# A fixed order for the first triangular inversion and the Gram products around it

## The chip, the cores and the metric

The kernel runs on one core of a Trainium2 chip. The metric is the device time of one execution in microseconds, the median of three runs. Engines are named TensorE (PE), VectorE (DVE), ScalarE (ACT), GpSimd (POOL) and SyncE (SP, which issues the DMAs).

## The reference

Three stages follow each other. The first is a gated delta rule over 768 tokens, for 4 batches of 8 heads with 48 features:

```
k_n = k / (|k| + 1e-6)
for t in range(768):
    y[t]  = q[t] @ state
    v_old = k_n[t] @ state
    state = state + beta[t] * outer(k_n[t], v[t] - v_old)
```

The outputs, 3072 tokens of 384 features, go through two dense blocks: `elu(x @ w_in) @ w_out`, and the same with a rational function P(h)/Q(h) in place of elu. The weights of both blocks arrive as float64 and are converted on the chip.

## The kernel before

**Windows.** The sequence is cut into 12 chunks of 64 tokens; two chunks make a window, so there are 6. For a window the kernel computes Gram products of keys and queries (`g_item`, line 270: four TensorE products into one of three PSUM buffers of the pool `pa`, a masked multiply on VectorE at L282 that keeps the query part, three copies on ScalarE at L286 to L288 that keep the key part; eight items per window). From the key part it inverts 32 x 32 triangular systems on VectorE (`t_pieces`): a transpose of the Gram matrix (L297, am<-gd), small steps on norms and beta (L301 to L333), 15 row steps, then four block steps px0 to px3 and four steps pt0 to pt3, each a product into `tmp` (L345) and a reduce (L346), and at the end a transpose (L372, tp_t<-tt). Then the recurrence over the chunks (`chain`) takes its turn: GpSimd multiplies tp_t with beta (L432, tb), TensorE solves (L460, L471, L483), ScalarE and VectorE copy and subtract (L463, L475, L488).

**Weights.** A conversion (`conv_x`, `conv_d`, `conv_s`) turns half a row block of float64 into fp32: two ScalarE steps (L160, L162), one or two VectorE steps (L176 to L179), a sign step on ScalarE (L180), a multiply on GpSimd (L182); for the first block's input weights a split follows on ScalarE (L71) and GpSimd (L72). There are two ce buffers between these steps, and eight raw buffers between the load (L142) and the conversion; a raw buffer is loaded again when GpSimd has done L182.

**Dense blocks.** For each window the first block runs its 16 slices (h_a at L578 to L580, o at L596 to L598), beside the next window's recurrence; behind the last window comes the second block.

**What sets the order.** Every piece is entered in a list with a number, its place in time: `at(t, fn)`. The list is sorted, and the pieces are emitted in that order. Pieces below `Q["ma"]` are emitted in a section whose order is kept on each engine, pieces above are handed to a scheduler that orders them by readiness under its own costs and puts them on the engines' queues, also between those of the fixed section. Window 0's Grams stand at -99 to -92, its inversion from -90 to -49, window 1's Grams from -72.1 to -63.3, the first conversions and the first recurrence from -48, -47 on. In before `ma` is -200, and nothing is below it.

Of the kernel before, what the change touches and what calls it, by code (L numbers as in the profile page):

```python
# [26 lines left out]
HD = DM // 2  # L27
NV = 15
Q = dict(
    ma=-200, xo=2.244, pg0=0, pg1=2, ca=0, g1=-72.135, g1d=1.259, t1a=-33.632, t1b=-8, npre=3, c0=-47,  # L30
    c0d=4.533, c1=-1.042, c1r=4.439, b1=0.704, c1o=0.919, h0=1.013, h0d=0.5, h1=0.586, h1d=0.462, g2=-7.824,
    g2d=1.116, g3w1=-0.578, g3=-0.806, t2=2.578, t2b=14.166, t3b=9, p=14.315, tm=4, chd=1.061, ws=0.808,
    sx=-0.529, ev=16.5, c5=1.1, c5d=0.4, l5=1.3, wu0=0, wl0=2, wd0=5, wy0=2, wm0=2, wu1=6, wl1=7, wd1=6, wy1=0,
# [4 lines left out]
def kernel(  # L38
# [520 lines left out]
    def g_list(w):  # L559
        return [(lambda j=j, s=s, b=b: g_item(j, s, b)) for j, s in enumerate(WINS[w]) for b in range(4)]  # L560
# [195 lines left out]
    def at(t, fn, *a):  # L756
        ev.append((t, len(ev), fn, a))

    def spread(t0, t1, fns, cost=None):
        cost = cost or [1.0] * len(fns)  # L760
        c = 0.0
        for fn, d in zip(fns, cost):
            at(t0 + (t1 - t0) * c / sum(cost), fn)
            c += d
# [33 lines left out]
    def t_at(w, t0, t1, t2, t3):  # L798
        tp = t_pieces(w)
        at(t0, tp[0])  # L800
        at(t0 + .3, tp[1])
        el = [4 * k * k for k in range(1, 8)] + [16 * k for k in range(8, 16)] + [1024, 768, 512, 256] + [256, 512, 768, 1024]
        spread(t1, t2, tp[2:-1], [.4 + .0021 * n for n in el])
        at(t3, tp[-1])
# [8 lines left out]
        at(-99 + i, fn)  # L813
    at(-91, chain_loads)
    at(10, coefs)
    t_at(0, -90, -85, -50, -49)
    for i, fn in enumerate(g_list(1)):
        at(Q["g1"] + Q["g1d"] * i, fn)
    at(-55, load_beta, 1)
# [8 lines left out]
    for w in range(NW):  # L828
# [15 lines left out]
        if w + 1 < NW:  # L844
            c0, cd = (Q["h0"], Q["h0d"]) if w == 0 else (Q["h1"], Q["h1d"])
# [150 lines left out]
```

## Time and profile before

| | |
|---|---|
| median of three runs | 1138.27 us (1136.64 to 1140.21) |
| the profiled execution | 1129.3 us, span 1127.5 us |
| TensorE busy | 1037.9 us, 92% of the span |
| VectorE busy | 904.5 us, 80% |
| ScalarE busy | 771.7 us, 68% |
| GpSimd busy | 466.4 us, 41% |

The profiled execution is shorter than the three timed ones; durations below are from it. A busy TensorE is not a TensorE at its peak, since the ends of its products are modelled. The share of busy time is a mean over stages: in the first 60 us TensorE is mostly idle and VectorE nearly full. An idle time in brackets is the time in which an engine waited in front of that row, with what ended the wait.

### The profile page before, as it was taken

The numbers are of one execution on the slowest core, as the hardware profiler recorded it, in microseconds if no ns is written. First come the engines' busy times: TensorE is split into PE (matmuls) and PEld (weight loads), VectorE is DVE, ScalarE is ACT, GpSimd is POOL, SyncE is SP. The second block draws the span as 40 slices with busy tenths as digits, with TensorE's granted clock in tenths as the row PEclk, the third lists the DMA queues.
The fourth block names the chain that finished last, engine by engine and source line by source line (L and its number), as shares of the span: only waits on it lengthen the run. The fifth ranks groups of instructions, "written<-read, shape, count | busy, mean of one in ns | idle before, by whom it ended". The sixth has DMA issues, their size and how long they took to land.

```text
span 1127.5 us, 20636 instructions
## 1 busy us (share of the span) xinstructions
PE 1037.9 (92%) x7952; PEld 835.8 (74%) x7952; DVE 904.5 (80%) x1240; ACT 771.7 (68%) x1525; POOL 466.4 (41%) x399
## 2 busy tenths in 40 slices
PE   7178898889798999899999999999999999999997
PEld 7155676667676778777888878778788888888885
DVE  4989889689857873795434379999999999999997
ACT  5568687866577546665665689976767667676764
POOL 1376655434332322242332145446363544536342
PEclk8559899999899989998999999999999999999999
DMA  9436343454364113120212044400100001010000
GB/s 287 155 102 200 116 147 114 131 161 126 97 189 149 59 50 121 60 81 1 81 49 62 1 148 133 120 28 1 56 1 25 32 1 56 1 56 1 29 1 28
DMA packets 51842, 91.75 MB, mean 81 GB/s; under 512 B 7072, under 2 KB 29728, under 8 KB 51744
## 3 DMA queue, kind: packets, MB, share of 16 engines
q1 hardware_dynamic: 51744, 90.43, 25.8%
q8 instruction: 62, 1.02, 0.4%
q14 instruction: 36, 0.29, 0.1%
HBM read 77.83 MB, written 12.58 MB: 80 GB/s over the span
## 4 chain that ended last, share of the span: by engine, by line
PE 54%; DVE 24%; ACT 7%; issue 6%; DMA 5%; POOL 3%; SPq 0%; ACTq 0%; DVEq 0%; POOLq 0%
PE o L733 13%; PE h_a L578 6%; PE h_a L579 6%; PE h_a L580 6%; DVE tmp L345 5%; PE o L596 3%; PE o L597 3%; PE o L598 3%; PE h_b L578 2%; PE h_b L579 2%; PE h_b L580 2%; DMA raw<-w_out 2%; DVE tt L346 2%; PE gp L279 2%; DVE wo L695 2%
## 5 line engine op out<-in xcount | busy, mean ns | idle before, releaser
L710 POOL TENSOR_TENSOR gl<-wo 128x1024 fp32r<-128x1024 f32 x47 | 147.3, 3134 | 202.4 <-DVE wo L709 174.2
L72 POOL TENSOR_TENSOR wor<-wo,wor 128x384 fp32r<-128x384 f32 x96 | 109.1, 1137 | 268.0 <-ACT wor L71 260.3
L578 PE MATMUL h_a<-xh,wi 128*128 128x512 f32 x417 | 173.9, 417 | 10.1 <-ACT pe L608 8.8
L579 PE MATMUL h_a<-xl,wi 128*128 128x512 f32 x417 | 168.9, 405 | 3.7 <-DVE xl L397 3.7
L580 PE MATMUL h_a<-xh,wi 128*128 128x512 f32 x417 | 167.8, 402 | 0.0
L733 PE MATMUL o<-gh,wo 128*128 128x512 f32 x564 | 135.9, 390 | 0.4 <-ACT ys L741 0.4
L613 DVE SCALAR_TENSOR_TENSOR e<-e,pe 128x512 f32<-128x512 f32 x96 | 70.8, 737 | 75.4 <-ACT e L609 75.1
L733 PEld LDWEIGHTS o<-gh,wo 128*128 128x128 f32 x564 | 105.2, 188 | 23.8 <-ACT ys L741 2.4
L596 PE MATMUL o<-gh,wor 128*128 128x512 f32 x288 | 115.8, 410 | 0.0
L597 PE MATMUL o<-gl,wor 128*128 128x512 f32 x288 | 114.5, 398 | 1.2 <-DVE gl L621 1.2
L598 PE MATMUL o<-gh,wor 128*128 128x512 f32 x288 | 113.0, 392 | 0.0
L578 PEld LDWEIGHTS h_a<-xh,wi 128*128 128x128 f32 x417 | 80.8, 194 | 30.5 <-ACT pe L608 10.9
L621 DVE TENSOR_TENSOR gl<-e,gh 128x512 fp32r<-128x512 f32 x88 | 79.2, 900 | 29.3 <-ACT gh L619 28.9
L579 PEld LDWEIGHTS h_a<-xl,wi 128*128 128x128 f32 x417 | 81.3, 195 | 22.1 <-DVE xl L397 7.2
L607 ACT ACTIVATE e<-h_a 128x512 f32<-128x512 f32 x91 | 54.2, 596 | 58.6 <-PE h_a L580 58.2
L580 PEld LDWEIGHTS h_a<-xh,wi 128*128 128x128 f32 x417 | 81.1, 194 | 17.3
L696 ACT ACTIVATE wo<-wo 128x1024 f32<-128x1024 f32 (+1 forms) x49 | 51.3, 1046 | 60.4 <-DVE wo L695 60.4
L619 ACT ACTIVATE gh<-e 128x512 fp32r<-128x512 f32 x96 | 60.0, 625 | 35.0 <-DVE e L613 35.0
L695 DVE SCALAR_TENSOR_TENSOR wo<-wo 128x1024 f32<-128x1024 f32 (+1 forms) x49 | 73.1, 1492 | 4.5 <-ACT wo L688 4.4
L71 ACT ACTIVATE wor<-wo 128x384 fp32r<-128x384 f32 x96 | 50.4, 525 | 35.7 <-PE o L598 35.3
L733 PE MATMUL o<-gl,wo 128*128 128x512 f32 x282 | 71.7, 389 | 0.8 <-POOL gl L710 0.8
L707 DVE SCALAR_TENSOR_TENSOR gh<-wo,ab_sb 128x1024 fp32r<-128x1024 f32 (+1 forms) x49 | 65.5, 1336 | 6.6 <-ACT wo L697 0.6
(168 smaller groups left out, 2462.8 us busy)
## 6 DMA issues: line engine op xcount, KB each, us to landing
kv<-c_kv SPq DMA_DIRECT2D x24, 576.0 KB, 4.6
gin<-g_in SPq DMA_DIRECT2D x69, 192.0 KB, 2.9
kq<-c_kq SPq DMA_DIRECT2D x22, 512.0 KB, 3.8
raw<-w_out SPq DMA_DIRECT2D x42, 192.0 KB, 2.5
raw<-w_in SPq DMA_DIRECT2D x34, 192.0 KB, 2.4
wo<-w_in SPq DMA_DIRECT2D x30, 192.0 KB, 2.7
xr<-x2d SPq DMA_DIRECT2D x6, 768.0 KB, 5.3
out_t<-ys SPq DMA_DIRECT2D x18, 256.0 KB, 2.2
```

The costliest lines, as they stand in the source:

```text
L72: eng.tensor_tensor(out=t[:, 1], in0=src, in1=t[:, 0].bitcast(F32), op=ALU.subtract)
L578: mm(out=ps, lhsT=hi, rhs=xh[:, c, 0:NC], start=(c == 0), stop=False)
L579: mm(out=ps, lhsT=hi, rhs=xl[:, c, 0:NC], start=False, stop=False)
L580: mm(out=ps, lhsT=lo, rhs=xh[:, c, 0:NC], start=False, stop=(c == 2))
L596: mm(out=ps[:, 0:NC], lhsT=hi[:, cs], rhs=gh[:, 0:NC], start=(f == 0), stop=False)
L597: mm(out=ps[:, 0:NC], lhsT=hi[:, cs], rhs=gl[:, 0:NC], start=False, stop=False)
L598: mm(out=ps[:, 0:NC], lhsT=lo[:, cs], rhs=gh[:, 0:NC], start=False, stop=(f == NF - 1))
L613: nc.vector.scalar_tensor_tensor(out=e, in0=e, scalar=-1.0, in1=p, op0=ALU.add, op1=ALU.add)
L621: eng.tensor_tensor(out=gl[:, 0:NC], in0=e, in1=gh[:, 0:NC].bitcast(F32), op=ALU.subtract)
L695: v.scalar_tensor_tensor(out=sq, in0=sq, scalar=1.0 + 1e-6, in1=ab, op0=ALU.add, op1=ALU.add)
L710: (v if k == NK - 1 else nc.gpsimd).tensor_tensor(out=gl, in0=sq, in1=ab, op=ALU.mult)
L733: mm(out=ps, lhsT=wo2[2 * j + i][:, int(p == 1), cs], rhs=(gl if p == 2 else gh)[:, n], start=(j == 0 and p == 0 and i == 0), stop=(j == N ...
```

## The change

Two numbers change. `ma` moves from -200 to -49.5, so that everything placed below -49.5 is emitted in the section with the kept order: the start, both windows' Grams, the first loads, and the first inversion. Its last piece, the transpose to tp_t, moves from -49 to -49.6, so that it is inside as well. Conversions and the recurrence stay with the scheduler.

```
-    ma=-200, xo=2.244, ...
+    ma=-49.5, xo=2.244, ...
...
-    t_at(0, -90, -85, -50, -49)
+    t_at(0, -90, -85, -50, -49.6)
```

VectorE, among the row steps of window 0's inversion, in before: L345 and L346 are its products and reduces (the last numbers are their sizes), L282 the masked multiply of a Gram item of window 1.

```order
L345 TENSOR_TENSOR tmp<-tt,am 128x64
L346 TENSOR_REDUCE tt<-tmp 128x4x4
L282 TENSOR_TENSOR p<-gp,cm_sb 128x256
L345 TENSOR_TENSOR tmp<-tt,am 128x100
L346 TENSOR_REDUCE tt<-tmp 128x4x5
L345 TENSOR_TENSOR tmp<-tt,am 128x144
L346 TENSOR_REDUCE tt<-tmp 128x4x6
L282 TENSOR_TENSOR p<-gp,cm_sb 128x256
L345 TENSOR_TENSOR tmp<-tt,am 128x196
```

The same place now:

```order
L345 TENSOR_TENSOR tmp<-tt,am 128x100
L346 TENSOR_REDUCE tt<-tmp 128x4x5
L345 TENSOR_TENSOR tmp<-tt,am 128x144
L346 TENSOR_REDUCE tt<-tmp 128x4x6
L345 TENSOR_TENSOR tmp<-tt,am 128x196
```

Seven of the eight multiplies of window 1 stood among the small steps and the row steps; now none does before the last row step (240 elements).

VectorE, from the third block step (px2, 512 elements) to the fourth (px3, 256) and on, in before: L179 is a conversion.

```order
L179 SCALAR_TENSOR_TENSOR ce<-wo_94 128x192
L346 TENSOR_REDUCE xx_t<-tmp 128x64
L179 SCALAR_TENSOR_TENSOR ce<-wo_94 128x192
L345 TENSOR_TENSOR tmp<-tt,am 128x256
L346 TENSOR_REDUCE xx_t<-tmp 128x64
L179 SCALAR_TENSOR_TENSOR ce<-wo_94 128x192
L345 TENSOR_TENSOR tmp<-xx_t,tt 128x256
L346 TENSOR_REDUCE tt<-tmp 128x16x4
L282 TENSOR_TENSOR p<-gp,cm_sb 128x256
```

The same place now, from the last multiply on:

```order
L282 TENSOR_TENSOR p<-gp,cm_sb 128x256
L345 TENSOR_TENSOR tmp<-tt,am 128x256
L179 SCALAR_TENSOR_TENSOR ce<-wo_94 128x192
L346 TENSOR_REDUCE xx_t<-tmp 128x64
L297 STREAM_TRANSPOSE am<-gd 128x1024
L345 TENSOR_TENSOR tmp<-xx_t,tt 128x256
L301 TENSOR_SCALAR x<-am 128x32
L179 SCALAR_TENSOR_TENSOR ce<-wo_94 128x192
L346 TENSOR_REDUCE tt<-tmp 128x16x4
```

The eight multiplies now stand from the 240-element row step to the 256-element block step, the last of them in front of the latter; four conversions stand in front of it in place of five. Window 1's transpose (L297) follows at once.

VectorE, around the end of the inversion (L372, tp_t), in before: L313 to L323 are window 1's small steps.

```order
L346 TENSOR_REDUCE tt<-tmp 128x16x4
L315 TENSOR_SCALAR t_432<-t_432 128x32
L179 SCALAR_TENSOR_TENSOR ce<-wo_94 128x192
L372 STREAM_TRANSPOSE tp_t<-tt 128x1024
L316 TENSOR_TENSOR rr<-rr,t_432 128x32
L179 SCALAR_TENSOR_TENSOR ce<-wo_94 128x192
L317 TENSOR_TENSOR t_432<-am,rr 128x32
```

The same place now:

```order
L346 TENSOR_REDUCE tt<-tmp 128x16x4
L318 TENSOR_SCALAR t_432<-t_432 128x32
L179 SCALAR_TENSOR_TENSOR wo_94<-wo_94 128x192
L372 STREAM_TRANSPOSE tp_t<-tt 128x1024
L319 RECIPROCAL rr<-t_432 128x32
L329 STREAM_TRANSPOSE n_t<-t_432 128x32
```

L316, L317 and L318 of window 1 now stand in front of tp_t, and 13 conversions in place of 11. Behind window 1's start the orders of all engines differ in a few places only; TensorE's is the same throughout but for six neighbouring products. On SP the two gin loads of window 1's last Gram item, which stood right behind the first eight weight loads, now stand behind a ninth, which waits for conversion 0 on GpSimd.

## Rows read from the trace of the kernel before

**Rows 1.** Page, chain that ended last: shares of the span by engine.
```profile
PE 54%; DVE 24%; ACT 7%; issue 6%; DMA 5%; POOL 3%; SPq 0%; ACTq 0%; DVEq 0%; POOLq 0%
```
**Rows 2.** Chain in order of time, 15 to 130 us: start, length, engine, tile, line.
```profile
17.57 1.96 DVE am L297
...
60.70 1.96 DVE tp_t L372
62.74 3.58 POOL tb L432 x4
...
121.96 1.98 DVE tp_t L372
```
**Rows 3.** Windows: stretch, its length, busy PE PEld DVE ACT POOL, clock, DMA.
```profile
40.00:50.00 10.00, 0.00 (x0) 0.00 (x0) 9.03 (x15) 7.16 (x26) 7.04 (x12) 0.50 0.46 138
```
**Rows 4.** Timeline of VectorE, 24 to 59 us: start, length, instruction, idle before it.
```profile
24.86 0.16 DVE L345 TENSOR_TENSOR tmp<-tt,am 128x4 f32<-128x4 f32 x1
24.94 0.42 DVE L282 TENSOR_TENSOR p<-gp,cm_sb 128x256 f32<-128x256 f32 x1
25.27 0.15 DVE L346 TENSOR_REDUCE tt<-tmp 128x4 f32<-128x4 f32 x1
...
36.00 0.41 DVE L345 TENSOR_TENSOR tmp<-tt,am 128x240 f32<-128x240 f32 x1
...
36.88 1.23 DVE L345 TENSOR_TENSOR tmp<-tt,am 128x1024 f32<-128x1024 f32 x1
38.14 1.22 DVE L346 TENSOR_REDUCE xx_t<-tmp 128x64 f32<-128x1024 f32 x1
39.28 0.35 DVE L179 SCALAR_TENSOR_TENSOR ce<-wo 128x192 int32<-128x192 int32 x1
39.54 0.95 DVE L345 TENSOR_TENSOR tmp<-tt,am 128x768 f32<-128x768 f32 x1
...
42.72 0.68 DVE L345 TENSOR_TENSOR tmp<-tt,am 128x512 f32<-128x512 f32 x1
43.88 0.73 DVE L179 SCALAR_TENSOR_TENSOR ce<-wo 128x192 int32<-128x192 int32 x1 [0.49 <-POOL wi L72]
...
46.16 0.41 DVE L345 TENSOR_TENSOR tmp<-tt,am 128x256 f32<-128x256 f32 x1
...
48.75 0.41 DVE L282 TENSOR_TENSOR p<-gp,cm_sb 128x256 f32<-128x256 f32 x1
...
56.56 1.96 DVE L345 TENSOR_TENSOR tmp<-xx_t,tt 128x1024 f32<-128x1024 f32 x1
```
**Rows 5.** Timeline of TensorE, window 1's Gram items and the first h_a.
```profile
21.70 3.78 PE L279 MATMUL gp<-xg 96*128 96x128 f32 x16 [1.93 <-DVE rr L316]
...
109.58 0.49 PE L578 MATMUL h_a<-xh,wi 128*128 128x512 f32 x1 [0.84 <-ACT xh L396]
```
**Rows 6.** Timeline of ScalarE, a Gram copy and a sign step.
```profile
20.82 0.27 ACT L286 ACTIVATE gd<-gp 64x128 f32<-64x128 f32 x1
...
46.32 0.36 ACT L180 ACTIVATE wo<-wo 128x192 f32<-128x192 f32 x1
```
**Rows 7.** Timeline of GpSimd, a conversion's last step.
```profile
46.49 0.60 POOL L72 TENSOR_TENSOR wi<-ce,wi 128x192 fp32r<-128x192 f32 x1 [0.47 <-DMA wo<-w_in]
```
**Rows 8.** DMA issues, 0 to 60 us: count, KB each, median us to landing.
```profile
wo<-w_out SPq DMA_DIRECT2D x5, 192.0 KB, 2.4
gin<-g_in SPq DMA_DIRECT2D x7, 192.0 KB, 5.1
```
**Rows 9.** Lines by form, VectorE, 19 to 63 us: busy, mean ns, idle before.
```profile
L316 DVE TENSOR_TENSOR rr<-rr,t 128x32 f32<-128x32 f32 x2 | 0.3, 168 | 0.0
L317 DVE TENSOR_TENSOR t<-am,rr 128x32 f32<-128x32 f32 x2 | 1.0, 478 | 0.0
```
**Rows 10.** Timeline of VectorE at 100.82; its waits in 132 to 142 (total, times, longest).
```profile
100.82 0.36 DVE L179 SCALAR_TENSOR_TENSOR wo<-wo 128x192 int32<-128x192 int32 x1 [0.64 <-ACT wo L162]
...
DVE ce L179 <- POOL wi L72: 3.7, 3, 2.1
```

More of the change, by code (lines that the diff above doesn't have):

```diff
@@ L29 @@
 Q = dict(
-    ma=-200, xo=2.244, pg0=0, pg1=2, ca=0, g1=-72.135, g1d=1.259, t1a=-33.632, t1b=-8, npre=3, c0=-47,
+    ma=-49.5, xo=2.244, pg0=0, pg1=2, ca=0, g1=-72.135, g1d=1.259, t1a=-33.632, t1b=-8, npre=3, c0=-47,
     c0d=4.533, c1=-1.042, c1r=4.439, b1=0.704, c1o=0.919, h0=1.013, h0d=0.5, h1=0.586, h1d=0.462, g2=-7.824,
```

## The prediction

> **What bounds the kernel now.** I read the chain of waits by engine first: TensorE holds 54% of it, VectorE 24% [rows 1]. TensorE is the bound of the long middle and end, which the change does not touch; the question is the head. The chain in order of time shows the head's course: VectorE transposes the Gram matrix at 17.57 us, works through window 0's triangular inversion, and ends with tp_t at 60.70 + 1.96 = 62.66; 0.08 later GpSimd begins the tb products that the first recurrence step needs, and VectorE's tp_t of window 1 is on the chain again at 121.96 [rows 2]. So nothing lies between the end of tp_t and the end of the kernel that would take up a delay by itself: a microsecond on tp_t is a microsecond on the end, unless a later wait shrinks. In the stretch 40 to 50 VectorE is busy 9.03 of 10 us and TensorE has nothing at all, at a granted clock of 0.50, the 1.2 GHz level [rows 3].
>
> **What moves.** Nothing is added or removed; two head sections get another order on VectorE, ScalarE, GpSimd and SP, and TensorE's order stays. The profiled execution took 1129.3 us (span 1127.5), the three timed runs have their median at 1138.27. I make the sum on the profiled execution and add the difference to the median, since the head's steps are the same in both.
>
> **1. The Grams of window 1 leave the row steps.** In before seven of their eight masked multiplies (L282) stand among VectorE's first steps. Two of them filled waits and cost nothing. Five stand between a product and its reduce: the product that begins at 24.86 ends at 25.02, the multiply goes in, the reduce begins at 25.27; without it, it would begin 0.03 later than the product's end. So 0.22 each, 1.1 us in all [rows 4]. In after the first of the eight stands before the 240-element product, which began at 36.00: it starts near 34.8.
>
> **2. They come back where TensorE has to be waited for.** Three PSUM buffers (pa) hold the Gram products. Items 0 to 2 of window 1 are done early, at 20 us. Item 3 needs item 0's buffer: its multiply (0.42), then three copies on ScalarE of 0.27 [rows 4, 6], so TensorE starts it at 34.8 + 0.42 + 0.85 = 36.1. At the 1.2 GHz level two items take 3.78, one 1.9 [rows 5]: items 3, 4, 5 and 6 end at 38.0, 39.9, 41.8 and 43.7. VectorE passes the 240 step, multiply 1, px0 (1.23 + 1.22) and multiplies 2 and 3 by 39.4 and one conversion by 39.6. It then waits 0.3 for item 4; px1 (0.95 twice) and multiply 5 end at 42.6; it waits 1.1 for item 6 and leaves it at 44.2. VectorE takes its instructions in order, so the inversion's px2, which needs none of this, stands behind these waits.
>
> **3. Three conversions in a row, with two ce buffers.** Behind px2's product come conversion 1, px2's reduce, conversions 2 and 3: to 45.1, 45.7, 46.0, and conversion 3 needs the buffer of conversion 1. That one's path: ScalarE is busy with the six copies of items 5 and 6 until 45.5, then one conversion step (0.36 long, 0.27 of it its own) and the sign step L180 to 46.05; GpSimd's L182 to 46.7, ScalarE's L71 to 47.1, GpSimd's L72 (0.60) to 47.8 [rows 6, 7]. Conversion 3 runs at 47.8, multiply 7 behind it, and px3 begins at 48.5. In before it began at 46.16 [rows 4]: +2.3 so far. Multiply 7 needs its own load: the two gin transfers go out when item 6 has freed their slots (43.7); with 2.4 us of landing, as a w_out load took in a quiet moment, and half an item on TensorE that is 47.1, so GpSimd is the later; with the 5.1 of gin's own median, most of it from the crowded start, it would be 49.8 [rows 8].
>
> **4. From px3 to tp_t.** Before: 46.16 to 62.66. After: one multiply less (0.42, 0.34 of it its own); a wait of 0.5 for conversion 4's buffer, by the same GpSimd path; three more conversions and three more of window 1's small steps in front of tp_t. A conversion takes 0.35 beside an idle GpSimd and 0.73 beside a busy one [rows 4], less the 0.08 by which it overlaps its neighbour: 0.27 to 0.65, I take 0.45 for GpSimd's half-busy state. The small steps take 0.17 to 0.48 by their groups [rows 9]; I take 0.33. So -0.34 + 0.5 + 1.35 + 1.0 = +2.5. The end of tp_t moves by 2.3 + 2.5 = +4.8, to 67.5. Bounds: without steps 2 and 3's waits (1.4 and about 1.8) and at the cheap prices (0.81 and 0.51), 4.8 - 3.2 - 1.0 = +0.6; with the late gin load (1.7) and the dear prices (1.95 and 1.44), 4.8 + 1.7 + 1.0 = +7.5.
>
> VectorE's two-input steps next to GpSimd are the dearest uncertainty. The 1024-element product takes 1.23 with GpSimd idle and 1.96 beside it, a reduce 1.22 [rows 4]. The Trainium skill, SBUF — State Buffer, "SBUF: two separate sides", has it that a VectorE instruction with two SBUF inputs and a reading GpSimd instruction exclude each other for a whole instruction, so that one of them waits all of the other. By that rule each of the six extra steps, at its cheap price, could wait a whole GpSimd step of 0.60 besides: 2.6 and 2.3 in place of 1.35 and 1.0, and the sum would end up to 2.5 higher, at 1145. The same rule spares the moved multiplies, which read PSUM, and the multiply of 0.41 at 48.75 beside a busy GpSimd agrees.
>
> **5. What follows tp_t.** By the first L475 (the recurrence's lower step) the changed order has done 17 conversions, as many as before, so VectorE enters window 1's inversion with the same work and all of it later. One piece comes back: the VectorE wait of 0.64 at 100.82, for a conversion step on ScalarE [rows 10], shrinks because ScalarE and GpSimd had the same work and more time. I take -0.6. Moved SP loads and the coefficient steps (L789, L790, some 0.3 us of VectorE) stay beside other work; if their cover is gone they cost that 0.3. Sum: +4.8 - 0.6 = +4.2: 1129.3 goes to 1133.5 as a profiled time, 1138.27 to 1142.5. About 0.3% (3.4 us) is what a measurement of this kernel can tell from no change.
>
> **Rivals.**
> *The delay is taken up, or the waits are short (0.30, same).* If TensorE's items are ready sooner or ScalarE's copies do not hold the sign step, the waits of steps 2 and 3 lose about half, 1.6, and the shift is 4.2 - 1.6 = +2.6, 1140.9. For it: VectorE's row wait on GpSimd in this stretch was only 0.49 in before [rows 4]. Against: in after the copies stand in front of the sign step on ScalarE. That the fixed order binds only the head and changes nothing measurable ends here too.
> *Conversions get ahead (0.18, faster).* In after 13 conversions stand in front of tp_t, 11 in before. At 132 to 142 VectorE waits 3.7 us for GpSimd's L72, thus for the pace of conversions [rows 10]. If the two that are ahead stay ahead until there, each worth two GpSimd steps and a wait of 0.47 (1.67) [rows 7], those 3.3 us go; with tp_t not late but 1.1 early (step 1 alone) the end comes at 1138.3 - 1.1 - 3.3 = 1133.9. It decides from the point where tp_t comes no later than before. Against: the waits of steps 2 and 3 have to vanish, and by L475 both orders have done 17, so the lead is gone by then.
> *The gin load is late (0.10, slower still).* It stands in SP's queue behind a w_out load that waits for conversion 0 on GpSimd, and it may take 5.1 [rows 8]. Then multiply 7 starts at 49.8 in place of 48.1: +1.7 more, 1144.2.
>
> **Numbers.** Forecast as worked out 0.42 (1142.5, its own range 1141 to 1145), rivals as above. Slower by over 0.3%: the forecast and the late load, 0.52; within 0.3%: 0.30; faster: 0.18. The unknown prices alone go from +0.6 to +7.5, 1138.9 to 1145.8, and the range reaches down into the faster case: 1135.5 to 1146.5.
>
> **What would show it.** In the profile after: multiply 0 of window 1 near 34.8 on VectorE; waits of VectorE for TensorE's gp (L279) of about 0.3 and 1.1 between 39 and 44; a wait of about 1.5 for GpSimd's L72 before the conversion in front of multiply 7; px3 near 48.5; tp_t ending near 67.5; the first h_a matmul, at 109.58 in before [rows 5], near 113.8; from there the same distances to the end. Wrong if tp_t ends by 64, or if it ends late and the first h_a matmul does not, or if that is late and the span is not.

## The result and the profile after

The changed kernel takes 1145.58 us (median of 22 runs, 1138.23 to 1151.95); the kernel before took 1136.06 on the same chip (22 runs, 1124.97 to 1141.74). The ratio is 1.0081, with a 95% interval of 1.0063 to 1.0100: slower by about 9.2 us. The forecast was slower by 4.2 us. The direction came out, and so did each step up to tp_t within about half a microsecond; the size did not. The time lies inside the stated range, 1135.5 to 1146.5, but by luck: the range was laid around a median of 1138.27 from three runs, which 22 runs put at 1136.06, and the range left room for 8.2 us above that, the prices alone for 7.5. The medians differ by 9.5.

The profiled execution of the changed kernel has a span of 1136.5 us against 1127.5. The chain of waits has nearly the same shares by engine [rows 1]:

```profile
PE 56%; DVE 25%; ACT 6%; issue 5%; DMA 4%; POOL 3%; SPq 0%; ACTq 0%; DVEq 0%; POOLq 0%
```

VectorE's timeline of the changed kernel, to be laid beside [rows 4] (start, length, instruction, idle time before it and what ended it):

```profile
34.24 0.41 DVE L282 TENSOR_TENSOR p<-gp,cm_sb 128x256 f32<-128x256 f32 x1
...
39.40 0.42 DVE L282 TENSOR_TENSOR p<-gp,cm_sb 128x256 f32<-128x256 f32 x1 [0.35 <-PE gp L279]
...
43.20 0.42 DVE L282 TENSOR_TENSOR p<-gp,cm_sb 128x256 f32<-128x256 f32 x1 [1.19 <-PE gp L279]
...
47.18 0.73 DVE L179 SCALAR_TENSOR_TENSOR ce<-wo 128x192 int32<-128x192 int32 x1 [1.82 <-POOL wi L72]
...
48.17 0.41 DVE L345 TENSOR_TENSOR tmp<-tt,am 128x256 f32<-128x256 f32 x1
49.06 0.73 DVE L179 SCALAR_TENSOR_TENSOR ce<-wo 128x192 int32<-128x192 int32 x1 [0.48 <-POOL wi L72]
...
56.55 0.74 DVE L179 SCALAR_TENSOR_TENSOR ce<-wo 128x192 int32<-128x192 int32 x1 [0.86 <-POOL wi L72]
...
65.67 1.94 DVE L372 STREAM_TRANSPOSE tp_t<-tt 128x1024 f32<-128x1024 f32 x1
```

The two waits for TensorE's Gram items (forecast 0.3 and 1.1), the wait of the third conversion for GpSimd (1.8), px3 at 48.17 (48.5) and the end of tp_t at 67.61 (67.5) are all there. The wait of 0.86 in front of the conversion at 56.55 was not in the sum. In before tp_t ended at 62.66 [rows 2]: +5.0. This execution began its first transpose (L297) at 17.06 instead of 17.57; counted from there the inversion's end is 5.5 later.

GpSimd's timeline of the changed kernel, behind the end of tp_t:

```profile
67.64 0.59 POOL L72 TENSOR_TENSOR wi<-ce,wi 128x192 fp32r<-128x192 f32 x1 [0.47 <-ACT wi L71]
68.28 0.63 POOL L182 TENSOR_TENSOR wo<-wo 128x192 f32<-128x192 f32 x1
68.87 3.46 POOL L432 TENSOR_TENSOR tb<-tp_t,bm 128x256 f32<-128x256 f32 x4
```

Two conversion steps now stand in GpSimd's queue ahead of the tb products, which begin 1.26 us after tp_t's end; in before they began 0.08 after it [rows 2]. That is 1.2 us more that the forecast did not have. TensorE's first full tb product of window 0 (its second group, of 22 products) starts at 72.39, where before had it at 66.36: +6.0.

Then comes the part that was not foreseen. It lies in the second of the two chunks that window 0's recurrence works through, called the second sub-chunk below. R is the right-hand side of a solve, which VectorE writes (L452); it comes in two halves, so there are two tb products on it (L460). TensorE's timeline there, first of the kernel before:

```profile
91.17 1.11 PE L460 MATMUL cb<-R,tb 64*64 64x48 f32 x16
...
92.98 1.49 PE L471 MATMUL cb<-R,lb 64*64 64x48 f32 x32
...
97.77 1.13 PE L483 MATMUL cb<-R,tb 64*64 64x48 f32 x16
```

and of the changed kernel:

```profile
97.60 1.91 PE L460 MATMUL cb<-R,tb 64*64 64x48 f32 x16 [1.41 <-DVE R L452]
...
100.86 2.41 PE L471 MATMUL cb<-R,lb 64*64 64x48 f32 x32
...
109.09 1.94 PE L483 MATMUL cb<-R,tb 64*64 64x48 f32 x16
...
122.59 0.50 PE L578 MATMUL h_a<-xh,wi 128*128 128x512 f32 x1
```

The same instructions take 1.6 to 1.7 times as long. What differs stands in the clock column of the windows (stretch, length, busy time of PE, PEld, DVE, ACT and POOL, granted clock, DMA share, GB/s); before:

```profile
98.00:104.00 6.00, 6.00 (x74) 3.50 (x72) 5.25 (x8) 5.54 (x18) 3.89 (x6) 1.00 0.42 127
```

and changed:

```profile
98.00:104.00 6.00, 6.00 (x51) 3.89 (x49) 4.06 (x9) 3.87 (x12) 3.08 (x5) 0.50 0.59 169
104.00:110.00 6.00, 6.00 (x35) 3.42 (x33) 4.37 (x8) 2.53 (x6) 0.59 (x1) 0.50 0.00 1
110.00:114.00 4.00, 4.00 (x18) 1.67 (x19) 1.07 (x2) 2.93 (x10) 1.36 (x2) 0.50 0.20 53
```

TensorE is busy all of the time in both, but at 1.2 instead of 2.4 GHz from about 97 to 114 in the changed kernel. From the second tb product's start to that of the last L483 product it needs 11.5 us instead of 6.6. The first h_a starts at 122.59 instead of 109.58 [rows 5]: +13.0. Some of it comes back later: around 300 to 340 the chain of waits of the kernel before waits for weights,

```profile
299.91 3.32 DMA raw<-w_out
...
308.78 4.17 DMA raw<-w_out
```

and that of the changed kernel, in the same part of the program, runs through the next inversion on VectorE instead,

```profile
300.73 2.38 DVE tmp L345
...
303.71 0.86 DVE tt L346
```

so that the lag falls from 14.1 us (tp_t of window 3, 294.9 to 309.0) to 11.5 (the next transpose L297, 353.1 to 364.6), to 10.4 at the last window's tp_t, and to 9.0 at the end.

### The profile page after: what moved, and what is told of

It reads as the page before. It is cut to its first block, busy times and chain, and to the rows that moved or that the text cites. A ratio compares the mean times of both kernels' runs of the same rounds, so it can differ in the third digit from the quotient of the medians.

```text
span 1136.5 us, 20639 instructions
## 1 busy us (share of the span) xinstructions
PE 1042.8 (92%) x7952; PEld 837.3 (74%) x7952; DVE 902.7 (79%) x1240; ACT 772.3 (68%) x1525; POOL 464.2 (41%) x399
## 4 chain that ended last, share of the span: by engine, by line
PE 56%; DVE 25%; ACT 6%; issue 5%; DMA 4%; POOL 3%; SPq 0%; ACTq 0%; DVEq 0%; POOLq 0%
PE o L733 13%; PE h_a L578 6%; PE h_a L579 5%; DVE tmp L345 5%; PE h_a L580 5%; PE o L596 3%; PE o L597 3%; PE o L598 3%; PE gp L279 3%; PE h_b L578 2%; PE h_b L579 2%; PE h_b L580 2%; DVE tt L346 2%; DMA gin<-g_in 2%; DVE e L613 2%
```

## The experiments

Two theories went in. A: the head is late by 5 to 6 us, and a late head brings TensorE's clock down in the second sub-chunk, for some 7 us more. B: the loss behind tp_t is waits of the new order of conversions, the clock only goes along. Ratios below are to the kernel before, run beside each on the same chip. In all of these kernels the scheduler, which orders by its own estimate, also moved instructions elsewhere in the program: laid beside that of before, VectorE's timeline, of some 1,180 rows, differs in 83 to 179 of them, where that of after differs in 74. So none of the edits below is alone in its kernel.

**Fillers in the changed kernel.** Fillers are matmuls that give TensorE something to do; they compute nothing that is used.

```diff
-                        warm(d["tb"][:, 0, 0], Q[f"wu{j}"])
+                        for _ in range(3 if j and hf == 0 else 1): warm(d["tb"][:, 0, 0], Q[f"wu{j}"])
```

> The changed kernel with two more filler matmul pairs on TensorE behind the first half's tb product of window 0's second sub-chunk (three instead of one), where TensorE stood idle for 1.41 us at 96.2 to 97.6 just before its granted clock fell from 1.00 to 0.50. They compute nothing that is used. Theory A (about 6 us of VectorE and POOL delay ahead of the second sub-chunk, then some 7 us because TensorE ran at 1.2 instead of 2.4 GHz from 97 to 114): the granted clock stays 1.00 there, the second tb product takes 1.1 us instead of 1.91, the first h_a starts near 116 instead of 122.6, and the kernel lands 3 to 6 us below the changed one, at +3 to +6 us over the kernel before. Theory B (the 7 us are waits that the new order of conversions brings, R late and POOL's queue, and the clock is only a companion): first h_a at 122 to 125, time as the changed kernel, +8 to +10.

Measured: 1140.70 (12 runs), ratio 1.0040 (1.0012 to 1.0068), half the loss. TensorE's timeline:

```profile
97.69 1.56 PE L460 MATMUL cb<-R,tb 64*64 64x48 f32 x16 [1.40 <-DVE R L452]
99.18 3.27 PE L385 MATMUL warm<-p,tb 128*32 128x384 f32 x6
102.38 1.14 PE L471 MATMUL cb<-R,lb 64*64 64x48 f32 x32
```

The fillers did not go where I had meant them: both halves' products are emitted first, so they stand behind the second one, and the idle 1.40 us stayed. The clock fell at 98 all the same but was back at 1.00 by 102, not 114; L471 takes 1.14 instead of 2.41. The first h_a started at 118.66, 3.9 earlier than in the changed kernel. With the same late R the products run faster at the higher clock and the first h_a comes earlier, so the clock is not only a companion, and B as an account of the whole falls.

**A late tp_t without the changed order.** The kernel before, its last transpose done three times:

```diff
-            nc.vector.transpose(
+            for _ in range(3 if w == 0 else 1): nc.vector.transpose(
```

> The kernel before with the last step of the first inversion, the transpose into tp_t, done three times in window 0, so that its reader on POOL starts 3.9 us later, and nothing of the changed kernel's fixed order. Theory A (a late tp_t brings TensorE's clock down in the second sub-chunk): first h_a 9 to 13 us later than before, a stretch of granted clock 0.50 after the second sub-chunk's first tb product, and +6 to +9 us in all. Theory B (the loss behind tp_t belongs to the new order of conversions): clock 1.00 there, first h_a 4 to 5 us later, +2 to +4 us in all.

Measured: 1138.92, ratio 1.0027 (0.9999 to 1.0054). VectorE ends tp_t at 66.04 and TensorE starts the full tb product 3.2 us later than before:

```profile
64.11 1.93 DVE L372 STREAM_TRANSPOSE tp_t<-tt 128x1024 f32<-128x1024 f32 x1
```
```profile
69.52 1.94 PE L460 MATMUL cb<-kv,tb 64*64 64x48 f32 x26 [0.78 <-POOL tb L432]
```

The clock fell in the second sub-chunk as in the changed kernel, and the first h_a came at 121.29, as A wanted, but the medians differ by only about 3 us, as B wanted. The profile and the median disagree, and this is where A as stated falls: a single profile of a pair does not show what the median shows.

**The kernel before, twice again.** So the first profile of before (1129.3, at the fast end of its runs) was put to the test with two more.

> The kernel before, profiled a second time. Its first profiled execution (1129.3 us, mean granted clock 0.954) is among its fastest: 35 executions have a median of 1136.2 us and clocks from 0.939 to 0.957, the slow ones those with the low clock. Theory A2 (the fall of TensorE's clock in the second sub-chunk is not made by a late tp_t alone; the kernel before has it too in a good part of its executions, so that one pair of profiles shows more than the change costs): if this execution takes over 1134 us, there is a stretch of granted clock 0.50 between 88 and 112, and the first h_a starts 6 to 10 us later than 109.6. Rival (the stretch belongs to the changed order alone): clock 1.00 from 88 to 110 and first h_a at 109 to 111 at any time of the execution; slower executions lose it later.

> The kernel before, profiled a third time; the same two theories. A2: over 1134 us goes with half-clock stretches in the second sub-chunk or in window 0's first passes; under 1131 us with none. Rival: clock 1.00 from 88 to 110 in any case.

Measured: 1139.22 and 1126.31. TensorE and the windows of the first:

```profile
65.92 1.94 PE L460 MATMUL cb<-kv,tb 64*64 64x48 f32 x22 [0.24 <-POOL tb L432]
...
91.17 1.31 PE L460 MATMUL cb<-R,tb 64*64 64x48 f32 x16 [1.60 <-DVE R L452]
...
97.55 1.94 PE L483 MATMUL cb<-R,tb 64*64 64x48 f32 x16
...
116.37 0.50 PE L578 MATMUL h_a<-xh,wi 128*128 128x512 f32 x1
```
```profile
98.00:104.00 6.00, 6.00 (x39) 3.95 (x39) 3.15 (x4) 2.51 (x6) 0.59 (x1) 0.50 0.05 10
```

and of the second:

```profile
66.53 1.94 PE L460 MATMUL cb<-kv,tb 64*64 64x48 f32 x22 [0.45 <-POOL tb L432]
...
109.77 0.50 PE L578 MATMUL h_a<-xh,wi 128*128 128x512 f32 x1 [0.84 <-ACT xh L396]
```
```profile
98.00:104.00 6.00, 6.00 (x75) 3.69 (x74) 5.25 (x7) 5.54 (x18) 3.79 (x5) 1.00 0.41 121
```

The kernel before loses the clock at the same place in one of three profiled executions, with the head as early as ever. The fall costs 6.6 to 6.8 us at the first h_a (116.37 against 109.77 and 109.58). It does not belong to the change alone; what the change may alter is how often it comes.

What went before the fall can be read on GpSimd, at the second kv step (L422) of the sub-chunk, which needs a load of c_kv. First of the kernel before in its first profile, then in the one that fell, then of the changed kernel:

```profile
87.01 0.94 POOL L422 TENSOR_TENSOR kv<-kv,n_t 128x384 f32<-128x384 f32 x1
```
```profile
87.21 0.83 POOL L422 TENSOR_TENSOR kv<-kv,n_t 128x384 f32<-128x384 f32 x1 [0.71 <-DMA kv<-c_kv]
```
```profile
93.64 0.83 POOL L422 TENSOR_TENSOR kv<-kv,n_t 128x384 f32<-128x384 f32 x1 [1.12 <-DMA kv<-c_kv]
```

Conversion steps stand behind it in GpSimd's queue, and the conversion that VectorE has in front of the second R waits for them: 0.34 and 0.35 us in the two profiles of before that kept the clock, 1.51 in the one that fell, 1.19 in the changed kernel. So in these profiles a load that is late for GpSimd goes with a late second R and an idle TensorE. No experiment moved the load alone, and among the other kernels the clock fell without this wait too.

**The changed kernel again.**

> The changed kernel, profiled a second time (its first profiled execution, 1138.2 us, is the fastest of 22 with a median of 1145.6). The head, up to the first tb product, has no chance in it if the replay was right: tp_t ends at 67.4 to 67.8 and the first tb product starts at 72 to 72.7 again. A2: the half-clock stretch of the second sub-chunk is there again or sits elsewhere between 88 and 130, and where the execution takes over 1142 us there is more of it than the 17 us of the first.

Measured: 1147.63. tp_t ends at 68.58 and the full tb product starts at 73.35, 0.8 and 0.7 past the forecast intervals (this execution's first transpose is 0.9 later too); the clock is 0.50 from about 97 to 114, the same 17 us, and the first h_a at 122.99. That an execution over 1142 us has more of the stretch did not come out here; and GpSimd's wait for c_kv is there again, 1.18. Against the execution of before that fell as well, the two profiles of after have the first h_a 6.2 and 6.6 later, about the head's delay. It does not stay at that: by window 2's tp_t the two are 0.8 and 5.0 behind it, and the spans are 1136.5 and 1145.8 against 1137.4. What becomes of the head's 6 us by the end these profiles do not show.

**One half: the inversion alone in a fixed order,** the Grams of window 1 left to the scheduler.

```diff
-    ... g1=-72.135, g1d=1.259, ...
+    ... g1=-49.4, g1d=0.2, ...
```

> The changed kernel with only the inversion in a fixed order: the Gram products of window 1 are left to the scheduler again, which puts 11 conversions ahead of tp_t on VectorE, as before, and not 12. Prediction's steps 1 to 4 (the Grams that moved ahead cost the waits on TensorE and push the conversions together): tp_t ends at 62 to 64 instead of 67.6, TensorE's clock stays 1.00 in the second sub-chunk, first h_a at 109 to 112, time -1 to +2 us against the kernel before. Rival (the fixed order of the inversion is itself the cost, through the conversions behind it): tp_t at 65 to 68, +4 to +9 us.

Measured: 1140.83, ratio 1.0037 (1.0006 to 1.0068). The head is as early as before's or earlier,

```profile
59.25 1.97 DVE L372 STREAM_TRANSPOSE tp_t<-tt 128x1024 f32<-128x1024 f32 x1
```
```profile
65.59 1.94 PE L460 MATMUL cb<-kv,tb 64*64 64x48 f32 x22 [0.24 <-POOL tb L432]
```

so the fixed inversion by itself delays nothing up to there: the +5.0 needs the Grams. (11 conversions stand ahead of tp_t here; the changed kernel has 13, not the 12 of the expectation.) Yet the kernel loses 4 us, nearly half of the change's loss, without a late head: the clock fell at 93 to 110, and the conversion ahead of the second R waited 2.37 us for GpSimd, whose L422 had waited 1.20 for c_kv. tp_t came even earlier than forecast, at 61.22; the clock, the first h_a (118.49) and the time went against the forecast, and the time fell to the rival whose condition, a late tp_t, was not there.

**The other half: the Grams in a fixed order,** the inversion from the last of them on left to the scheduler.

```diff
-    ma=-49.5, ...
+    ma=-63, ...
```

> The changed kernel with the other half of it alone: the Gram products of window 1 stay in their fixed place ahead of px0, and from the last of them on the inversion is left to the scheduler, as before. VectorE then has conversions singly between the px and pt steps instead of three in a row, and tp_t two rows earlier. Steps 2 and 3 of the prediction: the two waits for TensorE's Gram items (0.3 and 1.1 us) stay, the wait of the third conversion for POOL (1.8 us) goes; tp_t ends at 63.5 to 65.5 (before 62.7, changed 67.6), the first tb product starts 1 to 4 us later than before's 66.4, and the time lies +1 to +5 us above before. Rival (the whole delay comes with the Grams): tp_t at 67 to 68, +7 to +10.

Measured: 1142.85, ratio 1.0040 (1.0007 to 1.0073). VectorE:

```profile
43.49 0.43 DVE L282 TENSOR_TENSOR p<-gp,cm_sb 128x256 f32<-128x256 f32 x1 [1.19 <-PE gp L279]
...
47.53 0.73 DVE L179 SCALAR_TENSOR_TENSOR ce<-wo 128x192 int32<-128x192 int32 x1 [1.10 <-POOL wi L72]
...
63.83 1.98 DVE L372 STREAM_TRANSPOSE tp_t<-tt 128x1024 f32<-128x1024 f32 x1
```

The Grams' waits are there (0.34 and 1.19), the conversion's wait is 1.10 instead of 1.82 and not gone, and tp_t ends at 65.81, 0.3 above my interval: +3.1 of the 5.0 comes with the Grams and what they do to the conversions. The other 1.8 needs both halves; that it is the three conversions in a row and the places further down is argued, not shown.

**A third conversion buffer in the changed kernel.**

```diff
-            e = conv_t[key] = mp.tile([128, HD], F32, tag="ce", name="ce", bufs=2)
+            e = conv_t[key] = mp.tile([128, HD], F32, tag="ce", name="ce", bufs=3)
```

> The changed kernel with three conversion buffers instead of two on the way from VectorE to POOL. Step 3 of the prediction (the third conversion waits 1.8 us for POOL because there are two buffers): that wait is gone, px3 at 46.3 to 47 instead of 48.17, but more conversions stand ahead of tp_t, which ends at 65.5 to 67. Theory A: the total follows the clock of the second sub-chunk, +1 to +5 us over before if it stays at 2.4 GHz and +7 to +9 if it falls. Theory B: the total follows tp_t alone, 0 to 2 us below the changed kernel.

Measured: 1139.43, ratio 1.0031 (1.0002 to 1.0061).

```profile
47.63 0.73 DVE L179 SCALAR_TENSOR_TENSOR ce<-wo 128x192 int32<-128x192 int32 x1 [1.56 <-POOL wi L72]
...
65.72 2.00 DVE L372 STREAM_TRANSPOSE tp_t<-tt 128x1024 f32<-128x1024 f32 x1
```
```profile
71.17 1.94 PE L460 MATMUL cb<-kv,tb 64*64 64x48 f32 x22 [0.36 <-POOL tb L432]
```

The wait is not gone but moved by one: with room for a fourth conversion, VectorE takes it up and waits 1.56 there. tp_t ends at 67.72, as late as in the changed kernel, and the tb product gains only 1.2 us, from GpSimd's queue. The clock fell at 95 to 112 in its profile. That the median is still 6 us below the changed kernel's, more than the 1.2 us, neither theory said.

**Fillers in the kernel before,** the same edit as in the first experiment.

> The kernel before with two more filler matmul pairs behind the first half's tb product of window 0's second sub-chunk (as in the run with the changed kernel, where they cut the half-clock stretch from 17 to 3 us). They compute nothing that is used and take 1.7 us of TensorE. Theory A2 (the kernel before loses the clock there in many executions): the median comes down by 1 to 4 us, to 1132 to 1135, and the mean granted clock of its executions rises from 0.9485 to 0.951 or more. Rival (it does not lose it there): the median goes up by 0 to 2 us, the clock stays.

Measured: 1132.38, ratio 0.9958 (0.9932 to 0.9985); the mean clock was 0.949, under the 0.951 that A2 asked for. It looked like a version that beats both, so two went further and one repeated it. With fillers of 512 columns behind all eight px and pt steps (`wr=8, wr0=8` for `wr=3, wr0=4`):

> The kernel before with the two more filler pairs in the second sub-chunk (as b_warm, 1132.4 us), and fillers of 512 columns behind all eight px and pt steps of the first inversion instead of 256 columns behind the last three, so that TensorE has work from about 46 to 63. They compute nothing that is used. Theory A2 (time follows the stretches in which the granted clock is 0.50): if the clock reaches 1.00 before the tb product at 64 to 66 instead of at 84, the first sub-chunk's products take 1.1 instead of 1.9 us, the first h_a starts 4 to 9 us earlier, and the median falls to 1124 to 1130. Rival (the fillers only stand in the way, or the clock does not rise): tb product as late as before or later, 1132 to 1136.

Measured: 1134.80, ratio 0.9986 (0.9951 to 1.0020). With a third conversion buffer:

> The kernel before with the two more filler pairs (b_warm, 1132.4 us) and a third conversion buffer, which takes the wait for POOL out of the conversions that stand ahead of the second R on VectorE (0.3 to 1.6 us in the three profiles of before). If that wait is what leaves TensorE idle there, its idle time ahead of the second tb product of the second sub-chunk goes to under 0.3 us and the median falls another 1 to 3 us, to 1129 to 1131.5. Rival (the fillers have covered it already): 1132 to 1134.

Measured: 1136.38, ratio 0.9989 (0.9959 to 1.0018): neither of the two forecasts. And the same kernel again:

> The kernel before with two more filler pairs in the second sub-chunk, run again: its first comparison gave 0.9958 (0.9932 to 0.9985), but two kernels that hold the same fillers beside another edit came out level with before (0.9986 and 0.9989). If the gain is the fillers' own: 0.9935 to 0.998 and a median of 1131 to 1135 where before has 1136 to 1137. Rival (the first comparison was a favourable draw of clock stretches): 0.998 to 1.002.

Measured: 1134.81, ratio 1.0005 (0.9976 to 1.0033). The first gain did not repeat. The two comparisons of this kernel have a mean ratio of 0.998, so a gain of some 2 us is neither shown nor ruled out. In the four profiles of the kernel before with fillers the clock falls in the second sub-chunk as well, for 3 to 7 us instead of 17: fillers shortened the fall and did not prevent it. In the kernel with fillers in the head the windows show what became of them:

```profile
46.00:52.00 6.00, 5.30 (x11) 1.35 (x9) 5.93 (x10) 3.81 (x15) 4.58 (x7) 0.52 0.48 150
52.00:54.00 2.00, 1.03 (x2) 0.11 (x2) 2.00 (x3) 1.73 (x7) 1.25 (x2) 1.00 0.54 174
54.00:60.00 6.00, 3.78 (x4) 0.26 (x4) 6.00 (x8) 4.85 (x20) 3.41 (x5) 0.60 0.36 103
60.00:66.00 6.00, 2.43 (x7) 0.67 (x8) 5.96 (x18) 3.93 (x15) 5.18 (x6) 0.50 0.34 100
```

The clock came up to 1.00 at the end of a stretch with TensorE busy 5.30 of 6 us, was at 1.00 for some 3 us, and fell again as the fillers, which wait for VectorE's steps, left gaps (TensorE busy 3.78 and 2.43 of 6 us); the tb product ran at the 1.2 GHz level as before.

## Why the prediction was right in direction and wrong in size

**Step 1** held: multiply 0 at 34.24 (forecast 34.8; the execution's head began half a microsecond earlier). Of the five multiplies that it places between a product and its reduce, only one stood there; four stood between a reduce and the next product, at the same price. **Step 2** held: waits of 0.35 and 1.19 for 0.3 and 1.1. **Step 3** held: 1.82 for 1.8, px3 at 48.17 for 48.5. Multiply 7, at 47.84, waited for no load, so the rival of the late gin load is out. **Step 4** held in its end and less well in its terms: tp_t ends at 67.61 for 67.5, but with the head half a microsecond early; from its first transpose the delay is 5.5 for 4.8. The sum had one wait of 0.5 for a conversion buffer, and there were two, 0.48 and 0.86. The waits it rests on did not shrink, which rules out the delay being taken up ahead of tp_t, and tp_t is not early, which rules out the faster rival. The rule of the Trainium skill, SBUF — State Buffer, "SBUF: two separate sides", was worked out as up to 2.5 us more, with tp_t at about 70. That sum let each extra step wait a whole GpSimd step, which did not come; the prices of the rows were the nearer ones. The rule itself the trace does not contradict: a conversion beside a busy GpSimd cost 0.73 or 0.74 again, and the four of that length between 47 and 64 each began 0.07 or 0.08 after a GpSimd step L182 and ended 0.2 after it, as if they had waited for what was left of it:

```profile
47.10 0.59 POOL L182 TENSOR_TENSOR ce<-ce,wo 128x192 f32<-128x192 f32 x1
```


**Step 5** is the one that failed: "all of it later" and, in the last part, "from there the same distances to the end". Three things are in its place.

- GpSimd's queue: two conversion steps stand between tp_t and the tb products, 1.2 us. The forecast ended at tp_t, one engine short of its reader. Shown by the trace: tb product +6.0, in the second profile +7.0.
- The 0.6 us that were to come back did not. The wait of 0.64 for ScalarE [rows 10] is now this one, behind the slowed products:

```profile
112.93 0.36 DVE L179 SCALAR_TENSOR_TENSOR wo<-wo 128x192 int32<-128x192 int32 x1 [4.42 <-ACT wo L162]
```

- TensorE's clock. The forecast moved the second sub-chunk as it stood in one profile, at 2.4 GHz, and took it for a property of the kernel. Executions of one kernel differ in it. The fall costs 6.6 to 6.8 us at the first h_a; it was there in one of three profiles of before and in both of after.

How much each is worth in the median can only be estimated, in two ways. By profiles that fell alike the head alone is +6.2 to +6.6 at the first h_a. By all executions with a recorded clock, 97 of before and 22 of after: their mean granted clocks are 0.9479 and 0.9421, and within the kernels tried here an execution is 8.0 us (7.2 to 8.8) longer for each 0.01 of clock that it has less. At equal clock after is 4.2 us (3.0 to 5.4) longer than before; the other 4.6 are the 0.0058 of clock. The two ways do not cut at the same place: 6 us more of a head at 0.50 lower the mean clock by 6 x (0.948 - 0.5) / 1142 = 0.0024 by themselves, 1.9 us of the 4.6. So some 6 us would be the head and some 3 us more and longer half-clock stretches behind it.

This split is argued, not shown. The traces show the head's 6 us up to the first h_a and not to the end. The 97 executions were not run beside the 22, and groups of them taken at different times have mean clocks from 0.9462 to 0.9490, half of the difference that the split rests on. The fillers, which took 4.7 us from the changed kernel, were compared once there, and in the kernel before their gain did not repeat. With the fillers in both kernels, at equal clock, 4.2 us between them remain (+2.3 and -1.9 against before). The late tp_t by itself (+3.2 us on the tb product) cost 3.1 us with an interval from 0 to 6, which fits a head that is paid in full but does not show it.

Open is why the fixed inversion alone loses 4 us with its head on time, which the split above does not cover, and why a third buffer gives back 6 with tp_t as late. In their profiles (one each) the clock fell in the second sub-chunk, as in that of every kernel tried here with another order and no fillers. That before's order avoids the fall more often than others would fit; three profiles of it are too few to show it. A load of c_kv that comes late for GpSimd, as read above, is the nearest candidate for what decides it in before and after; that is not tested.

## What to carry to other kernels

Follow a delay to the engine that reads the late tile and through that engine's queue before calling it the price. Before working on a profile, see where its time lies among those of the other executions: here one of the shortest showed 2.4 GHz in a stretch where a longer one had 1.2, and the forecast built on it inherited that. And give a small gain a second comparison: 12 runs with an interval that left out 1 did not repeat.

## What the runs showed of the hardware

- The same program goes through the same work at either clock level from one execution to the next: 1.00 or 0.50 at 98 to 104, with TensorE busy 6.00 of 6 us in both. Ahead of the two tb products TensorE had stood idle 1.25 and 0 us in the first profile of before and 1.03 and 0.30 in the third, which kept the clock; 0.18 and 1.60 in the one that fell, and 0.87 and 1.41, 1.21 and 1.03 in the two of the changed kernel, which fell too. Both the sum and the wait for the second R are longer in the three that fell.
- The time of an execution follows its mean granted clock: in before, 97 executions from 1125.9 to 1145.8 us with clocks of 0.939 to 0.959 have a correlation of -0.84 between the two.
- A third buffer moved a wait and did not remove it: with two buffers the third of three conversions waited 1.82 us for GpSimd, with three the fourth waited 1.56.
